# A Performer attention with two dense layers: seven products for six more pairs of the first block

## The chip, the cores and the metric

The kernel runs on one core of one Trainium2 chip. The metric is the device time of one execution in microseconds, the median of several runs. Of the engines, PE (TensorE) multiplies, ACT (ScalarE) and DVE (VectorE) work element by element, POOL (GpSimd) does a few subtractions and issues some DMAs, and SP (SyncE) issues the other DMAs. Each engine takes its instructions in order; an instruction may wait on semaphores of the others.

## The reference

Linear attention with random features, then two dense layers over 2304 tokens of width 512 with 2048 features:

```python
q_p, k_p = (phi(q_s), phi(k_s))          # phi: exp(x @ omega.T - |x|^2/2 - max) / sqrt(m)
num = einsum('bhsm,bhmd->bhsd', q_p, einsum('bhsm,bhsd->bhmd', k_p, v))
x = num / (q_p . sum(k_p) + 1e-06)       # 2304 x 512
h = x @ w_in;  x = (max(h, 0) + alpha * min(h, 0)) @ w_out      # layer 0
h = x @ w_in2; x = (max(h, 0) ** 2) @ w_out2                    # layer 1
```

The weights come as 8-byte numbers and the products need more than one rounded factor, so the kernel splits every operand into a high part (fp32r) and the rest, and takes three matmuls per product: high by high, high by rest, rest by high.

## The kernel before, in words

Attention comes first: k steps, then q steps, which write the tokens x. Layer 0 then goes over 3 blocks k of 768 tokens, and in each over 8 pairs p of two groups of 128 features; one such pass is a *turn* (0 to 7 in block 0). A turn has first products, features and second products.

The **first products** h = w1 x of a pair are a 2 by 2 block product over halves of the width and of the block (i is the feature group, 384 tokens to a half). `plain` (L820) takes 8 products, `pair` (L870) takes Strassen's seven, whose right factors are quarters B of x or differences T1 to T4 of quarters, and whose left factors are quarters A of w1 or sums S1 to S4. `multiply` (L767) is one product: 6 matmuls of 384 columns. Block 0 uses `plain` for all of its pairs, blocks 1 and 2 use `pair`. The rounded quarters are xh (ACT, L439) and xl (DVE, L442).

The **features**: ACT copies h from PSUM to c, or to a scaled copy s that DVE then adds to another h (`c<-h,sg,s`, L805, in `pair` only); DVE bends c (L810); ACT rounds it to gh (L792); DVE takes the rest gl (L816).

The **second products** y = w2 g (`mm2`, L950, L963) of a pair are spread over the turn of the next pair: after the products of a turn come as many of ten parts as `FILL` says, first those of i=1 (gh and both parts of w2), then i=1 with gl, then i=0. In a plain turn the first part comes after the first product, in a turn of seven after the second.

The **weights** of block 0 are made while it runs, and stored for the later blocks. A *unit* n makes w1 of pair n and w2 of pair n-1 and lies in turn n-1. It has four raws (a and b for w1; p and q for w2, i=1 and i=0): POOL issues the DMA of the 8-byte words (`Raw`, L122); ACT scales the high word in place (`scale_high`, L132) and writes the scaled low word as 16-bit numbers (L141) and the high word as f16 (L142) into the two halves of `rest`; DVE shifts the high word to t (L146) and merges t and rest to wf (L150). DVE makes the sums S (L168); ACT rounds wf to w (L229), DVE takes the rest (L232), SP stores both. Units are divided into 18 stages, and at each product the kernel issues the stages that are due (`upto`), so that weight operations stand between feature operations in the queues of ACT and DVE. Raws of block 0 are read into the part of x that no token fills at the time, three at a time; a new DMA is issued when a raw is merged.

Of the kernel before, what the change touches and what calls it, by code (L numbers as in the profile page):

```python
# [12 lines left out]
I16 = mybir.dt.int16  # L13
# [7 lines left out]
P = 128  # L21
# [39 lines left out]
def tile_performer_moe(ctx, tc, qt, kt, qn, kn, vn, omt, w1i, w1o, al, w2i, w2o, out):  # L61
# [113 lines left out]
    def made():  # L175
# [93 lines left out]

        yield  # L270
        for n, (n1, n2) in enumerate(UNITS[:NPAIR + 1]):
# [3 lines left out]
            todo = [[] for _ in range(STAGES)]  # L275
            if n1:
# [5 lines left out]
                todo[3] += [lambda: merge(a)] + [b.scale_low] * (n < 2)  # L282
                todo[4] += [b.shift] + [b.scale_low] * (n > 1)
# [93 lines left out]
    tp = making_room.enter_context(tc.tile_pool(name="tp", bufs=1, side="right", reuse_waits="tile"))  # L377
    tiles["wf1"] = wb.tile([P, 8, QW], F32, name="wf1")
# [995 lines left out]
```

## Time and profile before

| | us |
|---|---|
| median of 3 runs | 878.29 |
| lowest and highest | 878.25, 878.85 |
| profiled execution | 878.17 |
| its span in the trace | 876.4 |

In the profiled execution PE is busy 870.8 us, DVE 666.5, ACT 518.3 and POOL 88.9, at the full granted clock throughout. Attention ends near 139 us; block 0 of layer 0 lies from about 125 to 261 us. All times of the trace are microseconds from the start of the span; a row of a timeline gives the start, the length, and in brackets how long the engine had been idle and what it had waited for.

### The profile page before, as it was taken

Reading aid. Unit: us, or ns where it says so; the run is one execution under the profiler, and the core shown is the slowest. Engines: PE = TensorE matmul, PEld = TensorE weight load, DVE = VectorE, ACT = ScalarE, POOL = GpSimd, SP = SyncE. Lnnn points to the kernel's source line nnn. Section 1 sums busy time; section 2 is a strip of 40 time slices with the busy share of each in tenths; the row PEclk is TensorE's granted clock in tenths of the full one; section 3 lists DMA queues with packets and bytes.
Section 4 is the critical chain, followed back from the end, with each engine's and each line's share of the span. In section 5 each row is a group of like instructions: output and inputs, shape, how many; then the busy total and the mean of one; then the engine's idle time right before and its main releaser. Section 6 shows DMA issues by size and latency. Waiting matters only on the chain.

```text
span 876.4 us, 17518 instructions
## 1 busy us (share of the span) xinstructions
PE 870.8 (99%) x6848; PEld 807.5 (92%) x6848; DVE 666.5 (76%) x1095; ACT 518.3 (59%) x1023; POOL 88.9 (10%) x134
## 2 busy tenths in 40 slices
PE   9999999999999999999999999999999999999998
PEld 7998889999999999999999999998899988999887
DVE  4778987787777677797887875669965699757685
ACT  6889896888866566677667643335423245333442
POOL 6642321111101000001000000000000000000000
PEclk9999999999999999999999999999999999999999
DMA  8544316788835899948999966767687687876873
GB/s 286 187 137 160 111 38 217 264 314 307 291 157 211 327 384 412 370 145 304 402 390 393 357 243 189 252 260 282 239 300 250 209 325 258 289 254 219 309 258 142
DMA packets 86898, 228.76 MB, mean 261 GB/s; under 512 B 6688, under 2 KB 19360, under 8 KB 81824
## 3 DMA queue, kind: packets, MB, share of 16 engines
q1 hardware_dynamic: 77248, 192.21, 61.1%
q0 software_dynamic: 9216, 33.56, 10.8%
q10 hardware_dynamic: 352, 1.87, 0.6%
q8 instruction: 54, 0.88, 0.4%
q14 instruction: 28, 0.23, 0.1%
HBM read 170.47 MB, written 57.15 MB: 260 GB/s over the span
## 4 chain that ended last, share of the span: by engine, by line
PE 97%; ACT 2%; DMA 0%; DVE 0%; issue 0%; ACTq 0%; POOLq 0%
PE h L767 30%; PE y L963 22%; PE sumc L1153 11%; PE spare L767 10%; PE suma L1153 9%; PE h L532 4%; PE o L578 2%; PE t L539 2%; PE t L652 2%; PE o L684 2%; PE t L671 1%; PE t L526 1%; ACT e L557 0%; DMA x<-in_w2i 0%; PE h L1153 0%
## 5 line engine op out<-in xcount | busy, mean ns | idle before, releaser
L767 PE MATMUL h<-xh,w 128*128 128x384 f32 x1040 | 295.3, 337 | 0.3 <-ACT s L792 0.3
L767 PEld LDWEIGHTS h<-xh,w 128*128 128x128 f32 x1040 | 190.9, 188 | 3.3 <-ACT s L792 0.7
L963 PE MATMUL y<-gh,w 128*128 128x512 f32 (+1 forms) x768 | 175.4, 337 | 0.1
L767 PE MATMUL h<-xl,w 128*128 128x384 f32 x520 | 174.6, 336 | 0.0
L963 PEld LDWEIGHTS y<-gh,w 128*128 128x128 f32 x768 | 131.1, 188 | 11.6 <-ACT gh L792 0.5
L963 PE MATMUL y<-gl,w 128*128 128x512 f32 (+1 forms) x384 | 103.4, 337 | 0.0
L1168 ACT CAST gh<-g 128x768 fp32r<-128x768 f32 x72 | 56.9, 833 | 74.1 <-PE suma L1153 33.1
L767 PEld LDWEIGHTS h<-xl,w 128*128 128x128 f32 x520 | 97.7, 188 | 2.7
L767 PE MATMUL spare<-xh,w 128*128 128x384 f32 x336 | 90.9, 334 | 0.0
L1153 PE MATMUL sumc<-w,gh 128*128 128x512 f32 (+1 forms) x296 | 76.6, 379 | 0.0
L1170 DVE TENSOR_TENSOR gl<-g,gh 128x768 fp32r<-128x768 f32 x72 | 65.7, 953 | 14.3 <-PE suma L1153 7.1
L963 PEld LDWEIGHTS y<-gl,w 128*128 128x128 f32 x384 | 67.5, 188 | 9.3
L792 ACT ACTIVATE c<-h,sg_sb 128x384 f32<-128x384 f32 x48 | 28.0, 583 | 59.1 <-PE h L767 59.0
L767 PEld LDWEIGHTS spare<-xh,w 128*128 128x128 f32 x336 | 61.3, 188 | 0.2
L1153 PEld LDWEIGHTS sumc<-w,gh 128*128 128x128 f32 x296 | 52.8, 189 | 9.3
L545 DVE TENSOR_REDUCE mx<-h 128x8 f32<-128x1024 f32 x36 | 44.1, 1224 | 21.7 <-PE h L532 21.2
L810 DVE SCALAR_TENSOR_TENSOR c<-c,al_sb 128x768 f32<-128x768 f32 x48 | 48.6, 1013 | 12.3 <-ACT c L792 12.3
L767 PE MATMUL spare<-xl,w 128*128 128x384 f32 x168 | 56.1, 334 | 0.0
L1153 PE MATMUL suma<-w,gh 128*128 128x512 f32 x216 | 52.4, 391 | 0.0
L792 ACT ACTIVATE gh<-c,sg_sb 128x768 fp32r<-128x768 f32 x48 | 45.1, 940 | 8.3 <-DVE c L810 8.0
L150 DVE CUSTOM_DVE_ANT_0 wf<-t,rest 128x1024 uint16<-128x1024 uint16 x58 | 40.0, 690 | 11.8 <-ACT rest L142 9.8
L1153 PE MATMUL sumc<-w,gl 128*128 128x256 f32 x280 | 48.5, 282 | 0.0
(112 smaller groups left out, 1480.3 us busy)
## 6 DMA issues: line engine op xcount, KB each, us to landing
w<-k SPq DMA_DIRECT2D x99, 512.0 KB, 5.1
w<-k SPq DMA_DIRECT2D x39, 1024.0 KB, 4.6
w<-k SPq DMA_DIRECT2D x26, 896.0 KB, 8.5
k<-ms SPq DMA_DIRECT2D x36, 512.0 KB, 7.4
k<-w SPq DMA_DIRECT2D x7, 1792.0 KB, 6.2
x<-in_w1i POOLq DMA_DIRECT2D x16, 512.0 KB, 4.4
x<-in_w1o POOLq DMA_DIRECT2D x16, 512.0 KB, 7.3
k<-w SPq DMA_DIRECT2D x16, 512.0 KB, 6.0
```

The costliest lines, as they stand in the source:

```text
L150: nc.vector.tensor_tensor(out=self.out.bitcast(I32), in0=self.t, in1=self.rest, op=ALU.add)
L532: nc.tensor.matmul(pj[:, j, c, :], raws[key][rows, c, :], om[rows], start=True, stop=True)
L539: nc.tensor.matmul(o[rows, 2 * c:2 * c + 2], sqt[:, c, rows], pick, start=True, stop=True, skip_group_check=True)
L545: nc.vector.reduce_max(out=mx, in_=pj, axis=AX.X)
L578: nc.tensor.matmul(acc[b][ms, g, k * W:(k + 1) * W], es[i][rs, h % 2, h // 2, ms], vas[i % 4][rs, h], start=first and k == 0, stop=last, s ...
L767: nc.tensor.matmul(out, w[:, u, a, cs], tiles[v, b][:, kc], start=start and kc == 0 and j == 0, stop=stop and kc == 1 and j == 2, skip_gro ...
L792: nc.scalar.mul(out=to, in_=of, mul=sg_sb[:, 2 * p + i:2 * p + i + 1])
L810: nc.vector.scalar_tensor_tensor(out=c, in0=c, scalar=slope, in1=c, op0=ALU.mult, op1=ALU.max)
L963: nc.tensor.matmul(y[a0 // 512][:, a0 % 512:a0 % 512 + a1 - a0], u[:, i, c * P:(c + 1) * P], v[:, i, ts], start=first and j == 0 and a0 % ...
L1153: nc.tensor.matmul(to[c] if v == 3 or banks else to[c][:, :QW], (l if v == 2 else h)[:, r, c * P:(c + 1) * P], both(r) if v == 3 else w[:, ...
L1168: nc.scalar.copy(out=h[:, r], in_=f[:, r])
L1170: nc.vector.tensor_tensor(out=l[:, r], in0=f[:, r], in1=h[:, r].bitcast(F32), op=ALU.subtract)
```

## The change

- **Turns 2 to 7 of block 0 use `pair`** (`whole` is n < 2), with the fill table of seven products. Turns 0 and 1 stay `plain`.
- **T1 to T4 of block 0** are made by POOL in place of quarters of x (`apart`, 128x768 each, at q steps 12 to 15), and rounded by ACT and DVE in turns 1 and 2 (`SPLIT`).
- **Units from 2 on** are no longer built from the 18 stages, but by `evenly`, which names what comes at each product (`STEPS`). A21 is not rounded any more, so one cast and one rest are 256 columns wide instead of 512.
- **The joined words**: `scale_low` writes the scaled low word as whole 32-bit numbers into one of two buffers, `joined` or `ma`, and `sign` then writes the f16 high word over the upper half of each. `sign` waits for that write.
- **Raws** of units from 2 on are read into the `ms` buffers instead of x (`blk` is None); the two of w2 of pair 0 go to a buffer of gl and to a new one, `rx`.
- Blocks 1 and 2 use one table `NEXT`, and issue their weight stages over 52 products instead of 50.

```diff
+APART = {12: 4, 13: 6, 14: 5, 15: 3}
 CAST = 11
 STAGES, SHORT = 18, 10
+STEPS = (2, 5, 7, 10, 12, 15, 17)
...
+            if Raw.count in places:
+                raw = places[Raw.count]
+            elif blk is None:
+                raw = tiles["double"][k].bitcast(I32)
+            else:
+                raw = x[:, blk].rearrange("p c n -> p (c n)").bitcast(I32)[:, k * 2 * DM:(k + 1) * 2 * DM]
...
-        def scale_low(self):
+        def scale_low(self, to=None):
 
             if self.beside:
                 nc.scalar.mul(out=self.low, in_=self.low.bitcast(U32), mul=2.0 ** -29)
                 return
-            self.rest = tp.tile([P, DM], I32, name="rest")
-            part = lambda dtype, n: self.rest.bitcast(dtype).rearrange("p (n w) -> p n w", w=2)[:, :, n]
-            nc.scalar.mul(out=part(I16, 0), in_=self.low.bitcast(U32), mul=2.0 ** -29)
-            nc.scalar.copy(out=part(F16, 1), in_=self.high.bitcast(F32))
+            self.rest = tiles["joined"] if to is None else to
+            nc.scalar.mul(out=self.rest, in_=self.low.bitcast(U32), mul=2.0 ** -29)
+            if to is None:
+                self.sign()
+
+        def sign(self):
+
+            part = self.rest.bitcast(F16).rearrange("p (n w) -> p n w", w=2)[:, :, 1]
+            nc.scalar.copy(out=part, in_=self.high.bitcast(F32))
...
+        def evenly(n, n1, n2, todo):
+
+            def put(step, *what):
+                todo[STEPS[step]] += what
+
+            joined = tiles["joined"], tiles["single"].bitcast(I32)
+            put(3 if n > 2 else 1, trail)
+            put(3, *[trail] * (n == 2))
+            if n1:
+                a, b = used[n, 0, 0], used[n, 0, 1]
+                put(0, a.scale_high)
+                put(1, lambda: a.scale_low(joined[0]), a.sign, a.shift, lambda: read_out(a))
+                put(2, lambda: merge(a), b.scale_high, lambda: b.scale_low(joined[1]), b.shift)
+                put(3, b.sign, lambda: read_out(b), lambda: cast1(n1, A11, S1))
+                put(4, lambda: merge(b), lambda: sums((1, 3)), lambda: sums((2, 4)), lambda: rest1(n1, A11, S1))
+            if n2:
+                p, q = (lambda: used[n, 1, 1]), (lambda: used[n, 1, 0])
+                put(3, lambda: p().scale_high())
+                put(4, lambda: p().scale_low(joined[0]))
+            if n1:
+                put(4, lambda: cast1(n1, A22, A11))
+            if n2:
+                put(4, lambda: p().sign(), lambda: p().shift(), lambda: read_out(p()), lambda: q().scale_high())
+            if n1:
+                put(4, lambda: cast1(n1, S1, S3), lambda: rest1(n1, A22, A11))
+                put(5, lambda: rest1(n1, S1, S3))
+            if n2:
+                put(5, lambda: q().scale_low(joined[1]), lambda: q().sign(), lambda: merge(p()),
+                    lambda: q().shift(), lambda: read_out(q()))
+            if n1:
+                put(5, lambda: cast1(n1, S3, 8))
+            if n2:
+                put(6, lambda: cast2(n2, 1))
+            if n1:
+                put(6, lambda: rest1(n1, S3, 8),
+                    lambda: keep(n1, 0, slice(0, 7), ring[n1[1] % 2][0][:, :, A22:]))
+            if n2:
+                put(6, lambda: merge(q()), lambda: rest2(n2, 1), lambda: cast2(n2, 0),
+                    lambda: tail.append(lambda: rest2(n2, 0)))
...
+            if n > 1:
+                evenly(n, n1, n2, todo)
+                n1 = n2 = None
...
+    INSTEAD = {T1: (0, 0), T3: (0, 1), T2: (1, 1), T4: (1, 0)}
+    SPLIT = {(1, 0): [(cast, T2)], (1, 1): [(rest, T2)], (1, 2): [(cast, T1)], (1, 3): [(rest, T1)],
+             (1, 4): [(cast, T3)], (1, 5): [(rest, T3)], (2, 1): [(cast, T4)], (2, 2): [(rest, T4)]}
+
+    def in_place(_, n):
+
+        return quarter(0, *INSTEAD[n])
+
+    def apart(n):
+
+        of = {T1: (T3, T1), T3: (T2, T3), T2: (T2, T1), T4: (T4, T2)}[n]
+        a, b = (in_place(0, m) for m in of)
+        nc.gpsimd.tensor_tensor(out=in_place(0, n), in0=a, in1=b, op=ALU.subtract)
...
+            places[4] = mp["gp"].tile([P, 2, NB], F32R, name="gl").rearrange("p i n -> p (i n)").bitcast(I32)[:, :2 * DM]
+            places[5] = rx.tile([P, 2 * DM], I32, name="rx")
...
+                    if s in APART:
+                        apart(APART[s])
...
-        first = (layer, k) == (0, 0)
-        steps = stepping.pop() if stepping else plain(p) if first else pair(layer, p)
+        first, whole = (layer, k) == (0, 0), n < 2
+        if n == 0:
+            ask(ENDS[0], None)
+        steps = stepping.pop() if stepping else plain(p) if whole else pair(layer, p)
...
+            for what, operand_ in SPLIT.get((n, m), ()):
+                what(0, operand_, in_place)
...
-            for _ in range(FILL[0 if first else 1][m]):
+            for _ in range(FILL[0 if whole else 1][m]):
```

The instructions on ACT in one turn in the middle of block 0, before (w_0, w_1: the two w1 and w2 buffers; c and gh with h: features):

```order
L792 ACTIVATE c<-h,sg_sb 128x384
L229 CAST w_0_101<-wf_99 128x512 x2
L141 ACTIVATE rest<-x 128x512
L142 CAST rest<-x 128x512
L229 CAST w_1_2695<-wf_100 128x512
L792 ACTIVATE gh<-c,sg_sb 128x768
L792 ACTIVATE c<-h,sg_sb 128x384
L132 ACTIVATE x<-x 128x512
L141 ACTIVATE rest<-x 128x512
L142 CAST rest<-x 128x512
L132 ACTIVATE x<-x 128x512
L792 ACTIVATE gh<-c,sg_sb 128x768
```

Here gh follows a single cast of w2 (`w_1_2695`), and the next raw's work stands between the two gh.

ACT in the changed kernel, from the end of one turn into the next (s: the scaled copy for `c<-h,sg,s`; ms: raws; L138, L146, L153 are scale_high, the low write and `sign`):

```order
L244 CAST w_0_104<-wf_101 128x512 x2
L864 ACTIVATE gh<-c,sg_sb 128x768
L864 ACTIVATE s<-h,sg_sb 128x384
L138 ACTIVATE ms_2698<-ms_2698 128x512
L864 ACTIVATE gh<-c,sg_sb 128x768
L146 ACTIVATE joined<-ms_2698 128x512
L153 CAST joined<-ms_2698 128x512
L864 ACTIVATE s<-h,sg_sb 128x384
L138 ACTIVATE ms_2699<-ms_2699 128x512
L146 ACTIVATE ma<-ms_2699 128x512
L153 CAST ma<-ms_2699 128x512
L244 CAST w_0_102<-wf_100 128x512
```

The casts of w2 (`w_0_104`) now stand directly ahead of gh, and all work on raws a and b comes behind it, with s between.

DVE in a middle turn before, from the first sum:

```order
L168 TENSOR_TENSOR wf_99<-wf_99 128x256 x4
L146 TENSOR_SCALAR t<-x 128x512
L150 ISA wf_100<-t,rest 128x1024
L232 TENSOR_TENSOR w_0_101<-wf_99,w_0_101 128x512
L810 SCALAR_TENSOR_TENSOR c<-c,al_sb 128x768
L232 TENSOR_TENSOR w_0_101<-wf_99,w_0_101 128x512
L232 TENSOR_TENSOR w_1_2695<-wf_100,w_1_2695 128x512
L146 TENSOR_SCALAR t<-x 128x512
L150 ISA wf_100<-t,rest 128x1024
L810 SCALAR_TENSOR_TENSOR c<-c,al_sb 128x768
```

Both merges (L150) come within a few rows of the sums, with two rests and a bend between.

DVE in the changed kernel, from the `c<-h,sg,s` after the fifth product to the one after the seventh:

```order
L877 SCALAR_TENSOR_TENSOR c<-h,sg_sb,s 128x384
L161 ISA wf_100<-t,ma 128x1024
L179 TENSOR_TENSOR wf_100<-wf_100 128x256 x4
L247 TENSOR_TENSOR w_0_102<-wf_100,w_0_102 128x512
L157 TENSOR_SCALAR t<-ms_2697 128x512
L247 TENSOR_TENSOR w_0_102<-wf_100,w_0_102 128x256
L247 TENSOR_TENSOR w_0_102<-wf_100,w_0_102 128x512
L161 ISA wf_101<-t,joined 128x1024
L157 TENSOR_SCALAR t<-ms_2698 128x512
L882 SCALAR_TENSOR_TENSOR c<-c,al_sb 128x768
L877 SCALAR_TENSOR_TENSOR c<-h,sg_sb,s 128x384
L247 TENSOR_TENSOR w_0_102<-wf_100,w_0_102 128x512
```

Behind `c<-h,sg,s` stand the sums, three rests and the merge of p.

The end of a turn in the changed kernel on DVE (the turn before the rows above), from the shift of q:

```order
L157 TENSOR_SCALAR t<-ms_2697 128x512
L882 SCALAR_TENSOR_TENSOR c<-c,al_sb 128x768
L877 SCALAR_TENSOR_TENSOR c<-h,sg_sb,s 128x384
L247 TENSOR_TENSOR w_1_103<-wf_100,w_1_103 128x512
L161 ISA wf_101<-t,ma 128x1024
L247 TENSOR_TENSOR w_0_104<-wf_101,w_0_104 128x512
```

The merges of p and q (L161 to `wf_101`) now stand behind the sums, three rests and a bend, at the turn's end.

## Rows read from the trace of the kernel before

**Rows 1.** The page, part 1: busy time and share of each engine.
```profile
PE 870.8 (99%) x6848; PEld 807.5 (92%) x6848; DVE 666.5 (76%) x1095; ACT 518.3 (59%) x1023; POOL 88.9 (10%) x134
```

**Rows 2.** PE timeline: start, length, engine, line, operation, names, shapes, count [idle before].
```profile
140.46 0.51 PE L767 MATMUL h<-xh,w 128*128 128x384 f32 x2
...
143.58 0.34 PE L767 MATMUL h<-xh,w 128*128 128x384 f32 x1
...
159.54 0.33 PE L767 MATMUL h<-xh,w 128*128 128x384 f32 x1
...
260.50 0.33 PE L767 MATMUL h<-xh,w 128*128 128x384 f32 x1
```

**Rows 3.** ACT timeline, end of turn 3 and start of turn 4 (same columns).
```profile
190.92 0.62 ACT L229 CAST w<-wf 128x512 fp32r<-128x512 f32 x1
191.43 0.94 ACT L792 ACTIVATE gh<-c,sg_sb 128x768 fp32r<-128x768 f32 x1
192.34 0.58 ACT L792 ACTIVATE c<-h,sg_sb 128x384 f32<-128x384 f32 x1
192.82 0.67 ACT L132 ACTIVATE x<-x 128x512 f32<-128x512 f32 x1
...
194.08 0.76 ACT L142 CAST rest<-x 128x512 f16<-128x512 f32 x1
194.70 0.68 ACT L132 ACTIVATE x<-x 128x512 f32<-128x512 f32 x1
195.28 0.92 ACT L792 ACTIVATE gh<-c,sg_sb 128x768 fp32r<-128x768 f32 x1
```

**Rows 4.** ACT groups, 30 to 500 us: busy us, mean ns | idle before.
```profile
L137 ACT ACTIVATE x<-x 128x512 int32<-128x512 uint32 x4 | 3.0, 758 | 0.0
```

**Rows 5.** DVE groups by line and shape, 30 to 500 us.
```profile
L805 DVE SCALAR_TENSOR_TENSOR c<-h,sg_sb,s 128x384 f32<-128x384 f32 x45 | 27.7, 615 | 13.6 <-PE h L767 5.1 <-ACT s L792 5.0 <-ACT ms L229 2.3
...
L232 DVE TENSOR_TENSOR ma<-wf,ma 128x256 fp32r<-128x256 f32 x15 | 6.3, 419 | 1.8 <-ACT ma L229 1.8
```

**Rows 6.** DVE timeline of turns 3 and 4.
```profile
192.18 0.42 DVE L146 TENSOR_SCALAR t<-x 128x512 int32<-128x512 int32 x1
192.64 0.69 DVE L150 CUSTOM_DVE_ANT_0 wf<-t,rest 128x1024 uint16<-128x1024 uint16 x1
193.25 1.01 DVE L810 SCALAR_TENSOR_TENSOR c<-c,al_sb 128x768 f32<-128x768 f32 x1
194.18 1.01 DVE L816 SCALAR_TENSOR_TENSOR gl<-c,sg_sb,gh 128x768 fp32r<-128x768 f32 x1
...
195.67 0.69 DVE L150 CUSTOM_DVE_ANT_0 wf<-t,rest 128x1024 uint16<-128x1024 uint16 x1
196.45 0.43 DVE L146 TENSOR_SCALAR t<-x 128x512 int32<-128x512 int32 x1
196.79 1.01 DVE L816 SCALAR_TENSOR_TENSOR gl<-c,sg_sb,gh 128x768 fp32r<-128x768 f32 x1
...
200.83 0.69 DVE L232 TENSOR_TENSOR w<-wf,w 128x512 fp32r<-128x512 f32 x1 [0.42 <-ACT w L229]
201.44 1.55 DVE L168 TENSOR_TENSOR wf<-wf 128x256 f32<-128x256 f32 x4
```

**Rows 7.** ACT timeline, turn 1: its first weight operation.
```profile
143.81 0.67 ACT L132 ACTIVATE x<-x 128x512 f32<-128x512 f32 x1
```

**Rows 8.** POOL timeline: one L521 of a q step, and the DMA after attention.
```profile
114.95 1.04 POOL L521 TENSOR_TENSOR sqt<-raw 128x512 f32<-128x512 f32 x1 [3.21 <-PE t L539]
...
141.57 0.55 POOL L122 DMA_DIRECT2D x<-in_w1o  x1 [0.30 <-POOL wf L154]
```

**Rows 9.** DMA issues from 120 to 260 us: count, KB each, median us to landing.
```profile
x<-in_w1o POOLq DMA_DIRECT2D x14, 512.0 KB, 7.6
x<-in_w1i POOLq DMA_DIRECT2D x12, 512.0 KB, 4.0
```

**Rows 10.** ACT groups from 143 to 261 us: rounding a token quarter.
```profile
L439 ACT CAST xh<-x 128x768 fp32r<-128x768 f32 x2 | 1.6, 824 | 0.0
```

More of the change, by code (lines that the diff above doesn't have):

```diff
@@ L12 @@
 F16 = mybir.dt.float16
-I16 = mybir.dt.int16
 I32 = mybir.dt.int32
@@ L100, in tile_performer_moe @@
     tiles = {}
+    places = {}
     class Raw:
@@ L196, in merge, with read_out @@
             raw.merge()
+            if raw in raws:
+                read_out(raw)
+        def read_out(raw):
             raws.remove(raw)
@@ L281, in made @@
                 todo[2] += [a.shift, b.scale_high]
-                todo[3] += [lambda: merge(a)] + [b.scale_low] * (n < 2)
-                todo[4] += [b.shift] + [b.scale_low] * (n > 1)
+                todo[3] += [lambda: merge(a), b.scale_low]
+                todo[4] += [b.shift]
                 todo[5] += [lambda: merge(b), lambda: cast1(n1, A11, S1)]
@@ L303, in made @@
                 todo[10] += [lambda: raw(0).scale_high()]
-                todo[11] += [lambda: raw(1).shift()] + [lambda: raw(0).scale_low()] * (n < 2)
+                todo[11] += [lambda: raw(1).shift(), lambda: raw(0).scale_low()]
                 todo[12] += [lambda: merge(raw(1))]
-                todo[13] += [lambda: raw(0).scale_low()] * (n > 1)
                 todo[14] += [lambda: cast2(n2, 1)]
@@ L1033, in tile_performer_moe @@
             if first and turn:
-                upto((p + 1) * STAGES + STAGES * (m + 1) // 8 + 1, ENDS[0], 0)
-            elif layer == 0 and k and turn * 7 + m > (0, 5, 3)[k]:
-                upto(end_of(ENDS[k - 1]) + (end_of(ENDS[k]) - end_of(ENDS[k - 1])) * (turn * 7 + m - (0, 5, 3)[k]) // (0, 50, 49)[k],
+                upto((p + 1) * STAGES + STAGES * (m + 1) // (8 if whole else 7) + 1, ENDS[0], None)
+            elif layer == 0 and k and turn * 7 + m > 3:
+                upto(end_of(ENDS[k - 1]) + (end_of(ENDS[k]) - end_of(ENDS[k - 1])) * (turn * 7 + m - 3) // (0, 52, 49)[k],
                      ENDS[k], k)
-            elif layer == 0 and k and m == (0, 5, 3)[k]:
+            elif layer == 0 and k and m == 3:
                 ask(ENDS[k], k)
             elif (layer, k, turn) == (0, 1, 0) and m < 2:
-                onward(ENDS[0], 0)
-            for blk, at in ((n // NPAIR, turn * (8 if first else 7) + m), (n // NPAIR - 1, NPAIR * 7 + turn * 7 + m)):
-                table = NEXT[0 if blk == 0 else 1]
-                at -= (NPAIR - 1) * (8 if blk == 0 and first else 7)
-                if blk == 0 and not first:
-                    at += 1
+                onward(ENDS[0], None)
+            for what, operand_ in SPLIT.get((n, m), ()):
+                what(0, operand_, in_place)
+            for blk, at in ((n // NPAIR, turn * 7 + m), (n // NPAIR - 1, NPAIR * 7 + turn * 7 + m)):
                 if 0 <= blk < BLOCKS:
-                    for what, operand_ in table.get(at, ()):
+                    for what, operand_ in NEXT.get(at - (NPAIR - 1) * 7, ()):
                         what((blk + 1) % BLOCKS, operand_)
```

21 lines of the change are left out of this document (8 added, 13 removed).

## Prediction

> **What bounds the kernel now.** I read the page's first part, then PE's timeline in block 0 of the first layer, then the timelines of ACT and DVE beside it. PE is busy 870.8 of 876.4 us [rows 1], and in block 0 its rows follow each other without a gap [rows 2]: 18 matmuls of 384 columns from 140.46 to 143.58, 0.1733 us each, and six turns from 159.54 to 260.50, 16.83 us each. So before the change a matmul removed is time gained, as long as PE stays dense. The profiled execution is 878.17 us, the median 878.29; I sum against 878.2.
>
> **What the change takes from PE.** A plain turn has 8 products of 6 matmuls, a turn of seven products has 7. Six turns (pairs 2 to 7) lose 6 matmuls each: 6 x 0.1733 = 1.04 us, so a dense turn becomes 15.79 us, and all six are worth 6.24 us. The order of the changed program has these 36 matmuls less, so this gain is there if PE never waits. The question is whether ACT and DVE can now make weights and features in 15.79 us per turn.
>
> **The ring of ACT and DVE.** In the new order both engines serve weights and features alternately, in order. Two waits close a ring in every turn from 3 to 7. ACT's copy s of the fifth product stands behind all its raw work of the turn; DVE's c<-h waits for that s, and behind it in DVE's queue stands the rest of the turn up to the merge of the last raw (q). ACT's cast of w for i=0 waits for that merge, and right behind that cast stands gh, which PE's first `y<-gh,w` of the turn needs. So one lap of the ring is the least length of a turn. I count start to start, from rows.
>
> ACT, from the cast of w (i=0) to the end of s: casts of w 0.51, gh 0.91, s 0.48, a scaling of high words 0.58, the old half-word f16 copy 0.62 [rows 3]. The new whole-word write of the low part: rows of the same form (L137) last 0.758 [rows 4]. Its f16 copy (`sign`) now waits for exactly that write, so the write counts with its whole length and a hand-over, 0.78, where today's 16-bit write gives way before its end. The lap: cast 0.51, gh 0.91, s 0.48, scale a 0.58, gh 0.91, low a 0.78, sign 0.62, s 0.48, scale b 0.58, low b 0.78, sign 0.62, cast A11 0.51, scale p 0.58, s 0.61 to its end = 8.95 us.
>
> DVE, from c<-h to the end of the merge of q: c<-h 0.615 long [rows 5], 0.53 start to start (other rows lose 0.08 to the overlap with the next); the merge of b 0.69 and 0.03, as the first sum waits for it; four sums 1.55 less 0.08 = 1.47; rests of 512 columns 0.61, of 256 columns 0.419 [rows 5] less 0.08 = 0.34; t 0.34 when nothing waits for it (196.45 to 196.79); a merge with a t that waits for it 0.78; bend 0.93 [rows 6]. The lap: 0.53, 0.72, 1.47, rest A11 0.61, t p 0.34, rest A22 0.34, rest S1 0.61, merge p and wait 0.78, t q 0.34, bend 0.93, c<-h 0.53, rest S3 0.61, merge q 0.72 = 8.53 us.
>
> Together **17.48 us per turn**, 1.69 more than the 15.79 of PE, and even 0.65 more than today's 16.83. PE itself is not in this lap: its fifth product ends 5.2 us after its first y (three products of 1.04, three fills of 0.69, which are 1536 columns each), ACT's s is due 7.5 us after. PE then stands once per turn, before its first `y<-gh,w`. Today there is no such ring: gh waits for a bend only, and ACT's casts and DVE's rests have the length of the turn.
>
> Is the wait of `sign` for its predecessor that dear on ACT? No row of before has an ACT instruction that waits for the one before it. On DVE there are such rows: the merge at 192.64 starts 0.46 after its t of 0.42, where t alone gives way after 0.34 [rows 6]. I take the whole length, and the other end is the 0.65 of today's low write (0.13 less, twice in a lap).
>
> The Trainium skill speaks for the dear end: Perfetto Trace Analysis, section "DVE / Act Engine Instruction (TENSOR_ADD, Activation, etc)", says that the end that the profiler reports is the acknowledged write with its semaphore update, so what waits for it cannot start inside the overlap. The DVE rows agree; for ACT no row does. By the page the total is the one below, by free overlap 1.5 us less.
>
> **Turn 1, where the new order begins.** The first raws of unit 2 were in x early: ACT scales the first at 143.81 [rows 7]. Now they go to ms, which is free only after the last attention step, so their DMAs start about where POOL's next one starts today, at 141.57 [rows 8], and words of w1i take 4.0 us [rows 9]: 145.6. ACT then has in its queue: scale 0.58, cast xh 0.74 (0.824 long [rows 10], less the overlap), gh 0.91, c 0.48, cast w 0.51, low 0.78, sign 0.62, xh 0.74, c 0.48, scale b 0.68 to its end: 152.1. DVE's t of b follows (0.34), then the new xl of T1 (about a bend, 0.87 to 0.93), then the rest of w for i=0 (0.69): 154.0. PE wants that rest at T1 = 142.71 (159.54 less one turn) plus five products (5.2) and six fills (4.2) and one matmul: 152.35. **Stall 1.65 us.** PE's sixth product, and with it ACT's third c, moves to about 155.9; ACT's nine operations behind it (c 0.48, low 0.78, A22 0.3, sign 0.62, scale 0.58, S1 0.51, low 0.78, sign 0.62, S3 0.61 = 5.3) and DVE's last rests and merges bring the merge of q to about 163.0. The rest of w (i=1) ends at 164.0, where PE wants it at 163.55: 0.5 us. Turn 2's lap has no first gh but one more xh, about 17.5; its gh is ready at 163.0 + 17.5 + 0.51 + 0.94 = 181.95, where PE is at 163.8 + 15.79 = 179.6: 2.35 us.
>
> **What is hidden.** POOL's four subtractions: L521's 128x512 takes 1.04 us [rows 8], so 1.56 at 768 columns; POOL has 3.21 us idle before each L521 of a step, and the results are wanted in turn 1. Cost 0, at most 0.5 us if one pushes a sqt. Casts and rests of T1 to T3 in turn 1 are in the sum above. The smaller A22 cast and rest (256 columns) are in the lap. SP has the same writes of kept weights. Turn 7 makes no first-product weights, so its lap lacks the merges of a and b, the sums and four rests (some 5 us), and gh of pair 7 is in time for turn 8. Blocks 1 and 2 keep their products, and their weight operations are spread over 52 steps instead of 50; `sign` costs ACT 0.13 for each raw there, and ACT is busy 518 of 876 us [rows 1]: 0.
>
> **Sum.** -6.24 + 1.65 + 0.5 + 2.35 + 4 x 1.69 (turns 4 to 7) = +5.0: **883.2 us**.
>
> **Bounds.** Without the wait of `sign`: -0.26 a turn, six turns, 881.7. Without the late DMAs of turn 1 as well, the first two stalls: -2.15, 879.5. Intervals of one form differ by some 0.03 between rows (scaling 0.58 and 0.61); were all 26 of a lap 2% shorter, -1.75 more: 877.8. Upwards: q's raw takes over a's buffer, so its DMA starts about 5 us into the lap and lands at 12.6 with 7.6 us for w1o [rows 9]. From then scale, S1, c and its write end at 14.3, DVE's bend wants c at 14.7. So up to 8.0 us it is hidden; every us beyond costs one per turn, 5 in all.
>
> **Rivals.**
> 1. The ring is not as tight as I count it, and PE stays dense: 878.2 - 6.2 = 872.0, and up to 876.5 with the stalls that begin in turn 1 (1.65, 0.5, 2.35). For it: ACT's and DVE's busy sums per turn (about 14.5 and 14.1 us by the same intervals) are under 15.79, so each engine alone would do. Against it: the lap would have to lose 1.7 of 17.48 us, 10%, in operations whose rows are constant to 0.03. Chance 0.15.
> 2. The lap comes out near 16.9 (no price for `sign`, every interval at its lower end): turns cost what they cost before, the gain of 6.24 is just eaten: 877 to 879.9. Chance 0.15.
> 3. The DMA of q is late in each turn, as it reads beside the writes of kept weights: at 9 us one us in each of five laps, +5, 888. Chance 0.05.
> 4. The program doesn't do what it says: excluded by the order, which has the 36 matmuls less.
>
> **How the numbers follow.** Forecast 883.2 (ring binds, 880.1 to 887.5): 0.65. A measurement of this kernel can tell some 0.2% from no change, so the bounds are 876.5 and 880.0. Faster 0.15 (rival 1), same 0.15 (rival 2 and the low end of the bounds), slower 0.70 (forecast and rival 3). The range leaves out rival 1 and rival 3: 876.6 to 887.5, which keeps 0.80.
>
> **What would show it.** Right: PE rows with idle time before the first `y<-gh,w` of turns 3 to 7, released by ACT's gh, about 1.7 us each, and one in turn 1 before an i=0 y, released by DVE's rest; turns of 17.5 us between first products of pairs; `sign` starting 0.78 after the low write. Wrong: turns of 15.8 us with PE dense (rival 1), of 16.8 (rival 2), or ACT's scale of q with idle time released by a DMA of in_w1o (rival 3). The forecast falls if ACT's gh is issued well before DVE's merge of q ends, since the ring has then another way round.

## The result and the profile after

The changed kernel takes **884.61 us** (median of 6 runs, 882.45 to 888.04), the kernel before beside it 878.95 us (6 runs, 878.25 to 879.29): **1.0069 times as long, 95% interval 1.0047 to 1.0091**. The forecast was 883.2 (876.6 to 887.5) and slower. The profiled execution of the changed kernel took 886.25 us, with a span of 884.5.

The first line of the page after, against [rows 1]: PE, DVE, ACT and POOL by busy us, share of the span, instructions.

```profile
PE 869.9 (98%) x6812; PEld 802.9 (91%) x6812; DVE 677.0 (77%) x1117; ACT 519.9 (59%) x1027; POOL 96.7 (11%) x138
```

PE has the 36 matmuls less. But busy time fell by only 0.9 us, not 6.24, and the span grew. In this execution PE ran for a while at half clock, which puts back 3.4 us (below), and busy time on this page contains modelled ends of matmuls, so a share of 98% does not say "dense". The timeline does. PE of the changed kernel: start, length, names, shapes, count, and the idle time before; the first y of turn 1, the rows in which PE had waited, and the first h of turns 2, 3 and 8.

```profile
147.85 0.86 PE L1035 MATMUL y<-gh,w 128*128 128x512 f32 x4
...
157.85 0.51 PE L1035 MATMUL y<-gh,w 128*128 128x512 f32 x1 [1.17 <-DVE w L247]
...
165.09 0.33 PE L839 MATMUL h<-xh,w 128*128 128x384 f32 x1
...
181.72 0.34 PE L839 MATMUL h<-xh,w 128*128 128x384 f32 x1
...
185.54 0.74 PE L1035 MATMUL y<-gh,w 128*128 128x512 f32 x2 [1.36 <-ACT gh L864]
...
202.60 0.73 PE L1035 MATMUL y<-gh,w 128*128 128x512 f32 x2 [1.06 <-ACT gh L864]
...
220.17 0.97 PE L1035 MATMUL y<-gh,w 128*128 128x512 f32 x4 [1.38 <-ACT gh L864]
...
237.20 0.97 PE L1035 MATMUL y<-gh,w 128*128 128x512 f32 x4 [1.02 <-ACT gh L864]
...
255.13 0.96 PE L1035 MATMUL y<-gh,w 128*128 128x512 f32 x4 [1.37 <-ACT gh L864]
...
268.88 0.33 PE L839 MATMUL h<-xh,w 128*128 128x384 f32 x1
```

Once per turn PE stands before the same instruction, the first `y<-gh,w`, and always for ACT's gh; in turn 1 it stands for DVE's rest of w. From one such y to the next it is 17.06, 17.57, 17.03 and 17.93 us. The six turns 2 to 7 take 268.88 - 165.09 = **103.79 us, where before took 100.96** [rows 2]; 6 x 15.79 would have been 94.7. PE's two largest waits from 140 to 270 us, by who was waited for (total us, times, longest):

```profile
PE y L1035 <- ACT gh L864: 6.2, 5, 1.4
PE y L1035 <- DVE w L247: 1.2, 1, 1.2
```

And why gh is late: ACT in the lap from 201.09 to 218.67 (same columns), and DVE's rows of the same lap.

```profile
201.09 0.62 ACT L244 CAST w<-wf 128x512 fp32r<-128x512 f32 x1 [2.04 <-DVE wf L161]
201.62 0.93 ACT L864 ACTIVATE gh<-c,sg_sb 128x768 fp32r<-128x768 f32 x1
...
204.30 0.68 ACT L146 ACTIVATE joined<-ms 128x512 int32<-128x512 uint32 x1
205.01 0.78 ACT L153 CAST joined<-ms 128x512 f16<-128x512 f32 x1
...
209.10 0.56 ACT L864 ACTIVATE s<-h,sg_sb 128x384 f32<-128x384 f32 x1
...
213.00 0.70 ACT L138 ACTIVATE ms<-ms 128x512 f32<-128x512 f32 x1 [0.96 <-DMA ms<-in_w1o]
...
218.67 0.62 ACT L244 CAST w<-wf 128x512 fp32r<-128x512 f32 x1 [1.62 <-DVE wf L161]
```

```profile
209.70 0.62 DVE L877 SCALAR_TENSOR_TENSOR c<-h,sg_sb,s 128x384 f32<-128x384 f32 x1 [1.85 <-ACT s L864]
...
214.22 0.69 DVE L247 TENSOR_TENSOR w<-wf,w 128x512 fp32r<-128x512 f32 x1 [0.43 <-ACT w L244]
...
217.95 0.69 DVE L161 CUSTOM_DVE_ANT_0 wf<-t,ma 128x1024 uint16<-128x1024 uint16 x1
```

This is the ring, read from one row to the next: the cast of w starts at 201.09, ACT works without a gap to the end of s at 209.66, DVE's c<-h has waited 1.85 us for it, DVE works on to the merge that ends at 218.64, and the next cast, which has waited for that merge, starts at 218.67 with gh right behind it. ACT's half is 8.57 us, DVE's 8.94. Of DVE's, 0.43 is a wait that begins on ACT (the row of 213.00): the words of q had not landed.

**A part that lies elsewhere.** The first y of turn 1 comes at 147.85. In the kernel before it starts at 143.76, behind the last h of [rows 2]'s first turn:

```profile
143.76 0.86 PE L963 MATMUL y<-gh,w 128*128 128x512 f32 x4
```

These 4.09 us arise in attention, where PE's order is the same in both kernels, and they have two sources. The larger one lies at 22 us. PE's row and the engines' busy time by stretches of 4 us (stretch, its length, busy us and instructions of PE, PE's loads, DVE, ACT, POOL, then the granted clock as a share of 2.4 GHz, DMA share, GB/s):

```profile
22.27 0.60 PE L599 MATMUL h<-om,raw 64*128 64x128 f32 x6 [0.68 <-issue]
```

```profile
20.00:24.00 4.00, 3.32 (x78) 2.91 (x74) 1.87 (x4) 3.81 (x13) 1.99 (x3) 1.00 0.48 149
24.00:28.00 4.00, 4.00 (x71) 3.69 (x69) 3.25 (x9) 3.00 (x10) 2.10 (x3) 0.64 0.71 208
28.00:32.00 4.00, 4.00 (x60) 3.76 (x60) 0.92 (x3) 2.57 (x9) 1.73 (x3) 0.51 0.32 87
```

PE paused for 0.68 us, and then ran most of two stretches at half clock, 1.2 GHz. By the granted clock 1.44 and 1.96 us of full speed are missing there ((1 - 0.64) x 4 and (1 - 0.51) x 4); with the pause that is 4.08. Row against row it is 4.05: PE is 0.43 ahead of the kernel before at 20.66 (there 21.09) and 3.62 behind it at 33.91 (there 30.29).

The smaller source is part of the change. POOL's first subtraction in place, one of DVE's xl beside it, and PE behind them:

```profile
102.58 1.81 POOL L526 TENSOR_TENSOR x<-x 128x768 f32<-128x768 f32 x1
```

```profile
103.50 1.70 DVE L501 TENSOR_TENSOR xl<-x,xh 128x768 fp32r<-128x768 f32 x1
```

```profile
107.08 1.06 PE L719 MATMUL t<-ident,eq 128*128 128x128 f32 x8 [0.42 <-DVE mx L618]
```

The three xl ahead of this one take 0.95 us each. This one, which starts while POOL subtracts, takes 1.70; the mx behind it comes late, and PE waits 0.42 us for it. From there on PE is 4.09 behind (108.08, there 103.99), 0.46 more than ahead of it. The kernel before has no such wait, and the traces of all the runs below have it. That the subtraction lengthens the xl is argued from these rows; no run takes it away.

The six executions have 882.45 us at a mean clock of 1.000, 883.09 at 0.999, 884.87 and 884.35 at 0.998, 886.25 at 0.996 and 888.04 at 0.994; the shortest, at full clock, is 4.2 us over the shortest of before. Turns 1 to 7 are 4.29 longer (122.07 from the first h of turn 1, 1.04 ahead of its first y, to that of turn 8; before 117.78), with the 0.46 in attention 4.75. So the change itself costs some 4.2 to 4.8 us; the rest of the 5.7 between the medians goes with the clock. For this reason the experiments below are compared by the stretch from the first h of turn 2 to that of turn 8, in which the granted clock was 1.00 unless something else is said: **103.79 in the changed kernel, 100.96 before**.

### The profile page after: what moved, and what is told of

It reads as the page before. It is cut to its first block, busy times and chain, and to the rows that moved or that the text cites. A ratio compares the mean times of both kernels' runs of the same rounds, so it can differ in the third digit from the quotient of the medians.

```text
span 884.5 us, 17465 instructions
## 1 busy us (share of the span) xinstructions
PE 869.9 (98%) x6812; PEld 802.9 (91%) x6812; DVE 677.0 (77%) x1117; ACT 519.9 (59%) x1027; POOL 96.7 (11%) x138
## 3 DMA queue, kind: packets, MB, share of 16 engines
q0 software_dynamic: 9216, 33.56, 11.3%
## 4 chain that ended last, share of the span: by engine, by line
PE 85%; ACT 7%; DVE 5%; issue 2%; DMA 1%; POOL 0%; ACTq 0%
PE h L839 24%; PE y L1035 17%; PE sumc L1225 11%; PE spare L839 10%; PE suma L1225 9%; PE h L599 4%; PE o L645 2%; PE t L606 2%; PE t L719 2%; PE o L751 2%; ACT gh L864 1%; DVE w L247 1%; ACT ms L138 1%; PE t L738 1%; DVE wf L161 1%
## 5 line engine op out<-in xcount | busy, mean ns | idle before, releaser
L839 PE MATMUL h<-xh,w 128*128 128x384 f32 x1016 | 287.2, 337 | 1.0 <-ACT s L864 0.6
L839 PEld LDWEIGHTS h<-xh,w 128*128 128x128 f32 x1016 | 186.3, 188 | 5.3 <-DVE c L877 1.4
L839 PE MATMUL h<-xl,w 128*128 128x384 f32 x508 | 170.4, 335 | 0.0
L839 PEld LDWEIGHTS h<-xl,w 128*128 128x128 f32 x508 | 95.5, 188 | 2.0
L877 DVE SCALAR_TENSOR_TENSOR c<-h,sg_sb,s 128x384 f32<-128x384 f32 x66 | 40.6, 615 | 27.1 <-ACT s L864 16.5
L864 ACT ACTIVATE s<-h,sg_sb 128x384 f32<-128x384 f32 x66 | 38.0, 576 | 32.6 <-PE h L839 32.5
L624 ACT ACTIVATE e<-h,nb 128x128 f32<-128x128 f32 x144 | 39.2, 382 | 16.8 <-DVE nb L619 16.7
```

Source lines behind the costliest of these rows:

```text
L624: nc.scalar.activation(out=e[:, c, :], in_=pj[:, c, :], func=AF.Exp, bias=nb[:, c:c + 1])
L839: nc.tensor.matmul(out, w[:, u, a, cs], tiles[v, b][:, kc], start=start and kc == 0 and j == 0, stop=stop and kc == 1 and j == 2, skip_gro ...
L864: nc.scalar.mul(out=to, in_=of, mul=sg_sb[:, 2 * p + i:2 * p + i + 1])
L877: nc.vector.scalar_tensor_tensor(out=c[:, ts], in0=b, scalar=sign, in1=s, op0=ALU.mult, op1=ALU.add)
```

## The experiments

Theory A is the prediction's: the lap of ACT and DVE through gh sets the turn. Its rivals: one engine has simply too much work; PE is dense and the loss lies elsewhere; the DMA of q sets the turn.

### Work doubled inside and outside the ring

Run e2_rest_twice_in_ring makes one rest of w (DVE, 0.61) twice within DVE's half of the lap:

```diff
-  put(4, ..., lambda: rest1(n1, A11, S1))
+  put(4, ..., lambda: rest1(n1, A11, S1),
+      lambda: rest1(n1, A11, S1))
```

> Edit: the rest of A11 (DVE, 512 columns, 0.61 us) is done twice, right where it stands: between the s of the fifth product and the merge of q. Ring theory: each lap grows by 0.61, turns 3 to 7 from 17.4 to 18.0, the stretch from turn 1 to turn 8 by 5 to 6 x 0.61 = 3.0 to 3.7 us to about 125.5. Rival (load): the same 3.7, so this run tells only together with the next. Rival (PE or the DMAs set the turn): 0.

Run e3_rest_twice_outside makes the same operation on the same engine, as often, behind the merge of q, where nothing on the way to gh waits for it:

```diff
-  lambda: tail.append(lambda: rest2(n2, 0)))
+  lambda: tail.append(lambda: (low(second(n2, 1, 0), f2[:, 0], second(n2, 0, 0)), rest2(n2, 0))))
```

> Edit: the rest of w2 for i=0 (DVE, the same operation and size, 0.61 us) is done twice where it stands, after the shift of b, where DVE then waits 1.85 us for ACT's s. Ring theory: the copy falls into that wait: 0, within 0.3 us in the whole stretch (122.1). Rival (load): +3.7, as for the copy in the ring.

The first h of turn 2 and of turn 8 on PE, first in e2, then in e3 (there with DVE's c<-h of the lap):

```profile
161.76 0.33 PE L840 MATMUL h<-xh,w 128*128 128x384 f32 x1
...
270.13 0.33 PE L840 MATMUL h<-xh,w 128*128 128x384 f32 x1
```

```profile
162.77 0.33 PE L839 MATMUL h<-xh,w 128*128 128x384 f32 x1
...
266.60 0.33 PE L839 MATMUL h<-xh,w 128*128 128x384 f32 x1
```

```profile
207.34 0.62 DVE L877 SCALAR_TENSOR_TENSOR c<-h,sg_sb,s 128x384 f32<-128x384 f32 x1 [1.12 <-ACT s L864]
```

Inside the ring: 108.37, 4.58 more. Outside: 103.83, 0.04 more, though DVE does as much: it waits for s all the same, only 0.7 us less than in the changed kernel. This pair alone puts "DVE has too much work" aside: **what counts is where the work stands**. That the inside one cost more than the 3.0 to 3.7 expected has two reasons in the rows (first y of three turns, a stretch of 3 us, and ACT's scaling of q in e2):

```profile
200.70 0.69 PE L1036 MATMUL y<-gh,w 128*128 128x512 f32 x1 [1.35 <-ACT gh L865]
...
219.05 0.97 PE L1036 MATMUL y<-gh,w 128*128 128x512 f32 x4 [0.84 <-ACT gh L865]
...
237.77 0.50 PE L1036 MATMUL y<-gh,w 128*128 128x512 f32 x1 [1.37 <-ACT gh L865]
```

```profile
201.00:204.00 3.00, 3.00 (x11) 2.82 (x11) 2.85 (x5) 2.85 (x5) 0.00 (x0) 0.50 1.02 429
```

```profile
230.60 0.68 ACT L138 ACTIVATE ms<-ms 128x512 f32<-128x512 f32 x1 [2.11 <-DMA ms<-in_w1o]
```

The bare lap is 17.04 (run e9 below), with one more rest 17.65. The lap from 200.70 took 18.35: a PE wait of 1.35 us was followed by a stretch at half clock. The lap from 219.05 took 18.72, at full clock: ACT waited 2.11 us for q's words.

### The ring cut

Run e1_cast_behind_gh keeps every operation and moves one: the cast of w for i=0 is issued in the next turn, behind gh and s, so that gh no longer stands behind a wait for DVE.

```diff
-  put(3 if n > 2 else 1, trail)
+  put(0 if n > 2 else 1, trail)
+  put(3, *[trail] * (n > 2))
...
-  ... lambda: cast2(n2, 0),
+  ... *([lambda: cast2(n2, 0)] if n == NPAIR else [lambda: tail.append(lambda: cast2(n2, 0))]),
```

> Edit: the cast of w2 for i=0 is issued in the next turn, behind gh and s, instead of ahead of gh; nothing else. Ring theory (gh waits for the merge of q, since that cast stands ahead of it): the wait of 1.0 to 1.4 us before the first y<-gh of turns 3 to 7 goes; ACT's part of the lap loses gh and s (0.84 + 0.46), so a lap is 17.40 - 1.3 = 16.1 us and bounds the turn weakly; turns 3 to 7 about 16.1, the stretch from turn 1 to turn 8 122.1 - 5 x 1.3 = 115.5 us, below the 117.8 of before. Rival (load: ACT and DVE have too much to do in a turn, wherever it stands): the wait moves to another place, the stretch stays at 122 within 1 us.

It took 879.87 us, and 99.99 in the stretch, 3.8 less than the changed kernel, where 6.6 were expected. PE's longest wait in total from 140 to 262 us:

```profile
PE y L1037 <- DVE w L247: 2.5, 6, 1.3
```

The wait for gh is gone altogether, so it was the cast ahead of gh that carried it. But the lap from 197.83 to 214.57 is still 16.74 us: the merge of q still releases that cast, and the cast an s further on in ACT's queue, and s the next merge. The ring is shorter, not open. The expectation had put this shorter lap at 16.1 us, and had left out that q's words come late here too: ACT waits 0.88, 0.97 and 0.67 us for them in three turns.

Run e5_ring_cut_twice takes away from ACT's half what stands ahead of the s of the fifth product as well: the cast of A11 and the scaling of p go behind it.

```diff
-  put(3, b.sign, lambda: read_out(b), lambda: cast1(n1, A11, S1))
+  put(3, b.sign, lambda: read_out(b))
+  put(4, lambda: cast1(n1, A11, S1))
...
-  put(3, lambda: p().scale_high())
-  put(4, lambda: p().scale_low(joined[0]))
+  put(4, lambda: p().scale_high(), lambda: p().scale_low(joined[0]))
```

> Edit: as in the run with the cast of w2 behind gh, and ACT's cast of A11 and the scaling of p stand behind the s of the fifth product instead of ahead of it. Ring theory: ACT's part of the lap between two merges of q loses 0.52 + 0.55 us, laps of 16.2 to 16.7 become 15.1 to 15.7, under PE's 15.79; PE dense but for 0.3 us a turn, so the stretch from turn 2 to turn 8, 103.8 in the changed kernel and 100.0 with the first edit alone, is 95 to 97 us. Rival (load: the same operations, so the same turns as with the first edit alone): 100.

878.89 us, 100.05 in the stretch: nothing won over e1, for two reasons. In turn 2 PE waits for ACT's c, and the turn takes 17.73 us instead of e1's 16.65. And turns 3 to 7 fall only from 83.34 to 82.32 (dense they would be 79); what ACT waits for from 160 to 262 us in e5 fits that. PE's row of turn 2, then ACT's wait:

```profile
163.70 0.45 PE L841 MATMUL h<-xh,w 128*128 128x384 f32 x1 [1.21 <-ACT c L866]
```

```profile
ACT ms L138 <- DMA ms<-in_w1o: 6.4, 5, 2.0
```

In the changed kernel the same wait was 1.2 us in all. With the ring cut, the raw of q is late in every turn: its transfer can start only when ACT and DVE have finished with a, whose buffer it takes.

Run e6_and_early_rest adds to e5 that in turn 1 the second of two pending rests of w is issued at step 1, not at step 3:

```diff
-  put(0 if n > 2 else 1, trail)
+  put(0 if n > 2 else 1, *[trail] * (1 if n > 2 else 2))
```

> Edit: as the run before, and in turn 1 the rest of w2 for i=0 is issued ahead of the shift of a, not behind the shift of b. Theory: PE's wait of 1.2 to 1.3 us in turn 1 goes (its cast is done 3 us before PE wants it), turn 1 from 18.3 to 17.0 us, the rest as in the run before; in all some 874 to 876 us against 878.3 of before, and runs that spread as little as those of before (0.1%), if the spread of the changed kernel (0.6%) comes from clock drops at its waits. Rival: turn 1 stays at 18.3 since ACT's late start moves the wait elsewhere.

Turn 1 fell to 16.82 us (18.29 in the changed kernel), the wait for DVE's w is gone, and the stretch is 99.92. In all 879.76 us (11 runs) against 878.70, ratio 1.0006 (0.9988 to 1.0023), where 874 to 876 were expected: the changed kernel with its ring cut twice and turn 1 mended is just the kernel before. The spread expected, 0.1%, did not come either: 877.03 to 881.43, at mean clocks of 0.999 and 1.000, so clock drops are not all of the spread.

### A fourth buffer for the raws

Run e9_changed_and_fourth takes the changed kernel as it is, and gives the raws of pairs 2 to 6 a fourth buffer (the room of ta and tb, two sums of token quarters that pairs 2 to 6 don't use).

```diff
-  raw = tiles["double"][k].bitcast(I32)
+  room = [*tiles["double"][:3], tiles["fourth"]]
+  raw = room[(Raw.count - 6) % 4 if Raw.count < 26 else (Raw.count - 26) % 3].bitcast(I32)
...
-  while order and len(raws) < 3 and ...:
+  while order and len(raws) < (4 if room[0] is None and Raw.count < 26 else 3) and ...:
```

> Edit: the changed kernel with the fourth buffer alone, order of ACT and DVE unchanged. Ring theory: laps lose only the two waits for the DMA (0.96 and 0.22 us, of which 0.5 and 0.2 show in a lap), laps of 17.0 instead of 17.0 to 17.9, the stretch from turn 2 to turn 8 103.8 - 0.5 to -1.5 = 102.3 to 103.3. If the DMA of q were what sets the turn: 97 or less.

886.06 us (with a pause and a low clock between 22 and 32 us, as above); the stretch is 103.22, as expected. PE's first y of two turns in e9:

```profile
202.80 0.50 PE L1036 MATMUL y<-gh,w 128*128 128x512 f32 x1 [1.04 <-ACT gh L865]
...
219.83 0.72 PE L1036 MATMUL y<-gh,w 128*128 128x512 f32 x2 [1.06 <-ACT gh L865]
```

The laps are now 17.04, 17.03 and 17.05 us, all alike. **17.04 is the bare ring**, and the half microsecond in some laps of the changed kernel was the DMA. The transfer was a small addition there, and the ring was the bound.

Run e11_a11_behind_s adds to e9 only the move of A11's cast and of p's scaling behind s; the cast of w stays ahead of gh.

```diff
-  put(3, b.sign, lambda: read_out(b), lambda: cast1(n1, A11, S1))
+  put(3, b.sign, lambda: read_out(b))
+  put(4 if n > 2 else 3, lambda: cast1(n1, A11, S1))
...
-  put(3, lambda: p().scale_high())
+  put(4 if n > 2 else 3, lambda: p().scale_high())
```

> Edit: the changed kernel with the fourth buffer, and in units from 3 on ACT's cast of A11 and the scaling of p behind the s of the fifth product; the cast of w2 stays ahead of gh. Ring theory: two operations of 0.52 and 0.55 us leave ACT's part of the lap, so the laps of 17.04 become 15.97, 0.18 above PE's 15.79; PE's wait before the first y<-gh falls from 1.0 to 0.2 us or less in turns 4 to 6, and the stretch from turn 3 to turn 7 from 68.7 to 64.4 us or a little less. Rival (it is the cast's place ahead of gh alone that counts): laps stay at 17.0.

878.53 us. First h of turns 4 to 7 on PE:

```profile
195.35 0.33 PE L841 MATMUL h<-xh,w 128*128 128x384 f32 x1
...
211.47 0.34 PE L841 MATMUL h<-xh,w 128*128 128x384 f32 x1
...
227.59 0.33 PE L841 MATMUL h<-xh,w 128*128 128x384 f32 x1
...
243.68 0.34 PE L841 MATMUL h<-xh,w 128*128 128x384 f32 x1
```

Turns of 16.12, 16.12 and 16.09, where 15.97 was expected: two operations of together about 1.1 us were taken out of the lap, and it lost 0.93. So the lap can be reckoned from its parts, here to within 0.15 us.

Run e8_fourth_buffer has all of it: e6, the fourth buffer, and for pair 2 the old place of A11 and p (in turn 1, ahead of the wait of turn 2 shown for e5).

> Edit: as the run with the ring cut twice and the early rest, and units 2 to 6 read their raws into four buffers instead of three (the fourth lies in ta and tb, which are free until turn 6), so that q's DMA is issued as soon as the q of the turn before is read; in turn 1 alone A11 and p keep their old place. Theory (after the cuts the DMA of q sets the turn: ACT waited 1.0 to 2.0 us for it in each of turns 2 to 6): those waits go, turns 2 to 6 fall from 15.7 to 17.8 to 15.8 to 16.1, the stretch from turn 2 to turn 8 from 100 to 96 to 97.5 (turn 7 still has three buffers), in all 875 to 877 us. Rival (ACT and DVE are still the lap): 100 as before.

**873.93 us (6 runs, 873.21 to 874.75) against 879.41: ratio 0.9933 (0.9916 to 0.9951).** It beats both kernels. PE's busy time in one turn, first of the changed kernel, then of e8 (columns as for the stretches above):

```profile
181.70:199.30 17.60, 16.24 (x92) 14.58 (x91) 14.86 (x27) 14.32 (x25) 2.47 (x5) 1.00 0.79 290
```

```profile
208.86:224.59 15.73, 15.73 (x92) 14.66 (x91) 14.35 (x26) 14.26 (x25) 1.58 (x3) 1.00 0.92 321
```

The same 92 matmuls in 15.73 us instead of 17.6, PE without a gap, while DVE and ACT are busy nearly as long. Four turns take 15.73 each, the stretch 95.69 (expected 96 to 97.5). Against e6, turn 2 gives 0.9 us of that (17.79 to 16.90; which of the two edits does it, no run tells), and turns 3 to 7, in which only the buffer differs, give 3.35 (82.14 to 78.79). The prediction's rival 1, 872.0, was out of reach for the changed kernel, not for its mathematics.

### The price of sign's wait

Run e7_half_words and run e10_half_words_and_fourth let the low write fill 16-bit halves, so that sign has nothing to wait for: e7 on the changed kernel, e10 on e9.

```diff
-  nc.scalar.mul(out=self.rest, in_=self.low.bitcast(U32), mul=2.0 ** -29)
+  nc.scalar.mul(out=self.rest.bitcast(I16).rearrange("p (n w) -> p n w", w=2)[:, :, 0], in_=self.low.bitcast(U32), mul=2.0 ** -29)
```

> Edit: the changed kernel, but the low part is written as 16-bit numbers into the lower halves as before, so that sign does not wait for it; buffers and order unchanged. By the prediction's price for that wait (0.13 us, twice in a lap, six turns) the stretch from turn 2 to turn 8 falls from 103.8 by 1.5; by the trace of the changed kernel (the write 0.71 from start to start, 0.65 today) by 2 x 0.06 x 6 = 0.7 us. If the wait were free: 0.

e7 decides nothing: 888.79 us, a stretch of 106.88, with a granted clock of 0.58 from 220 to 224 us, and longer waits for q's DMA, among which a gain of this size can't be read.

> Edit: the run before with half words, so that sign does not wait for the low write, now without DMA waits in between. Price of the wait by the trace: 2 x 0.06 us a lap, so 0.6 to 0.7 us less than the run before in the stretch from turn 2 to turn 8; by the prediction's 0.13 it would be 1.5.

e10, without those DMA waits and at full clock: 881.42 us, a stretch of 102.45, which is 0.77 less than e9 (expected 0.6 to 0.7). The same two waits of PE as shown for e9:

```profile
198.88 0.50 PE L1037 MATMUL y<-gh,w 128*128 128x512 f32 x1 [0.87 <-ACT gh L866]
...
215.79 0.73 PE L1037 MATMUL y<-gh,w 128*128 128x512 f32 x2 [0.93 <-ACT gh L866]
```

Laps of 16.88, 16.91 and 16.88 against 17.04: against the half-word write, the whole-word write with sign's wait costs 0.15 per lap, some 0.075 for each of two raws. It is not the price of the wait alone, since the two writes differ in length too (0.68 us as whole words, 0.79 as half words).

### The step-by-step order itself

Runs e4_stages and e4b_stages give pairs from 2 on the order of stages that pair 1 has, in place of the one placed step by step. In e4 a merge reads the joined words of the next raw, so its second-product weights aren't the reference's; e4b has the low write of q behind the merge of p instead.

```diff
-  if n > 1:
-      evenly(n, n1, n2, todo)
-      n1 = n2 = None
...
-  if n < 2:
-      todo[4] += [trail]
-      todo[7] += [trail]
+  todo[4] += [trail]
+  todo[7] += [trail]
```

> Edit: units from 2 on are built from the 18 stages as before, not step by step; products, differences by POOL, buffers of the raws and joined words stay as changed (with one joined buffer instead of two). gh then stands ahead of the cast that waits for the merge of q. Ring theory: no lap through gh, so PE's wait before the first y<-gh of a turn is under 0.3 us, turns of 15.8 to 16.5, the stretch from turn 1 to turn 8 113 to 117 us; against it, four merges in a row now share one joined buffer, which may make a lap of its own. Rival (load): 122 or more, since DVE and ACT have 0.2 to 0.3 us more to do in a turn (A21 is rounded again).

> Edit: units from 2 on built from the 18 stages, as in the earlier run, but the low words of q are written after the merge of p (in that run before it, so that p was merged with q's words). gh stands ahead of the cast that waits for the merge of q. By that run: PE no longer waits at y but 1.1 us a turn at the third product, for ACT's s, which now stands behind casts and low writes that wait for merges; the stretch from turn 2 to turn 8 about 104 to 106 us. Ring theory as I first had it (only the lap through gh counts): 96 to 98.

Both expectations failed. e4 took 886.96 us and 105.71 in the stretch (some 95 to 99 expected; its granted clock was 0.91 from 160 to 180 us), e4b 895.99 and 113.0 (104 to 106 expected; its granted clock was below 0.85 in several pieces of 4 us). PE's wait in e4 from 160 to 268 us (in e4b the same wait has 9.7 us), and one turn of e4b at full clock, from first h to first h (columns as above):

```profile
PE h L835 <- ACT s L860: 6.7, 5, 2.3
```

```profile
220.25:238.35 18.10, 16.27 (x92) 14.58 (x90) 14.70 (x26) 14.65 (x24) 2.11 (x4) 1.00 0.77 275
```

No wait for gh worth naming, but a longer one for s. What makes s late was not tested: ACT's waits for merges of joined words are short in e4b (3.0 us in nine), and there ACT also waits for PE's h (12.0 in five) and for DVE's bend (8.5 in seven). So "without this lap PE is dense" was too simple: these orders have other waits. Between the orders that give the reference's weights, the step-by-step one is the better: 17.05 to 17.57 us for turns 3 to 6 of the changed kernel, 18.10 for this turn of e4b.

## Why the prediction was right, point by point

**The gain of PE**: right. The forecast's dense turn was 15.79 us; e8's dense turns are 15.73. It is there whenever nothing makes PE wait.

**The ring**: right as a mechanism, and shown: e2 and e3 (position of the same work), e1 (the wait for gh goes with the cast ahead of it) and e11 (about 1.1 us taken out of it, 0.93 gained). Its size was 17.48 in the forecast; the bare ring is 17.04 (e9), with q's late words 17.57. The ACT half measured 8.57 instead of 8.95, DVE's 8.40 instead of 8.53 in a lap without DMA wait (227.25 to 235.65). Of ACT's 0.38, 0.15 lies in the two low writes and as much in the two gh, which give way after 0.84 and 0.83 us (201.62 and 203.47), not 0.91. So PE's waits before the first y were 1.02 to 1.38 us and not 1.7, and turns 3 to 7 took 17.05 to 17.92.

**The wait of sign**: the right kind; the write that it waits for was taken too long. The forecast took 0.78 from [rows 4] as the start-to-start time of the low write; it is 0.71, since here the write lasts 0.68 and not 0.758. sign starts at 205.01, when the write that began at 204.30 has ended at 204.98, where other rows of ACT start about 0.09 before their predecessor ends (cast and gh at 201.09 and 201.62). The Trainium skill, Perfetto Trace Analysis, section "DVE / Act Engine Instruction (TENSOR_ADD, Activation, etc)", has the reported end at the acknowledged write; the ACT rows agree. Against the half-word write it is worth 0.15 per lap (e10), where the forecast said 0.26: over six turns 0.77, not 1.5.

**Turn 1**: wait of 1.17 us, turn longer by 1.46 (18.29 against 16.83), forecast 1.65. e6 takes it away by an earlier rest, so it was DVE's rest indeed. The late start of the raws shows in ACT's first scaling of turn 1, and its releaser is the DMA, as forecast:

```profile
149.54 0.67 ACT L138 ACTIVATE ms<-ms 128x512 f32<-128x512 f32 x1 [1.54 <-DMA ms<-in_w1i]
```

The first y of this turn is itself 4.09 later than before, so this row is to be compared with 145.6 + 4.09 = 149.7.

**Turns 2 to 7**: turn 2 took 16.63, that is 0.84 over 15.79 (forecast 0.5, but as a wait for DVE's rest, which PE's rows don't have there), turns 3 to 7 together 8.21 over (forecast 2.35 + 4 x 1.69 = 9.11). With turn 1 the excess is 10.5, forecast 11.3. One part had no term: the last lap, up to turn 7's first y, is 17.93 (in e9 too), because DVE then also makes the quarter sum tb between a shift and a bend:

```profile
249.98 0.95 DVE L491 TENSOR_TENSOR tb<-x,ta 128x768 f32<-128x768 f32 x1
```

**POOL's subtractions**: priced at nothing, or 0.5 us if one pushes a sqt. They last 1.81 to 2.26 us instead of 1.56. By the rows above they cost PE some 0.46 us (argued, not tested), by a way that was not asked about: the xl of DVE beside the first of them.

**The DMA of q**: the step that failed, though it moved the total little. The forecast let the landing be hidden up to 8.0 us from its issue, as only DVE's bend was asked about. The rest of S1 stands ahead of that bend, by the forecast's own intervals at 12.96 us of the lap, and a landing at 12.6 ends S1's cast at 13.8: by the same reckoning the cover was 6.8 us. POOL issued it 5.0 us into the lap, as forecast:

```profile
206.08 0.53 POOL L128 DMA_DIRECT2D ms<-in_w1o  x1 [6.61 <-DVE gl L888]
```

But ACT wanted the words at 212.04, 5.96 us later, and got them at 213.00; right behind that scaling stands the cast of S1, whose rest on DVE waited 0.43. So the cover was some 6.5 us (6.92 to the landing less 0.43), not 8.0, and from there DVE's half grows; where ACT waited 0.22 for q's words (at 246.88), DVE's rest did not wait. And the forecast treated it as a rival to the ring; it is the next bound behind it (e5, e6): cutting the ring a second time won 1.0 us in turns 3 to 7, and the buffer 3.35 more (e8).

**The sum**: +4.29 over turns 1 to 7, forecast +5.0; with the 0.46 in attention 4.75. The medians differ by 5.66, and the longer executions are those with a lower clock, for which the forecast had no term. So a part of its closeness to the time is luck: the bare ring was priced 0.44 per lap too long, and q's late words, tb, the subtraction and the clock, none of them in the sum, made up for it.

**What stays open**: why PE pauses at some 22 us with nothing to wait for in the profile, and why only some of these pauses bring a low clock: e3 has one of 0.62 us without. Whether the change has a part in it no run here tells. The kernel before has executions with a low clock too, as one of 882.42 us at a mean clock of 0.996 and one of 885.82 at 0.992, but no trace of one was kept.

## What to carry to other kernels

Where two engines take turns in order, list who waits for whom once around and add the start-to-start times of one lap: if the lap is longer than the work of the engine that bounds the kernel, it can be the time, as it was here, though both engines were idle for a sixth of it. To test for it, do one operation twice, once inside the lap and once beside it. When the lap is cut, look for what was late behind it: here a transfer, for which a fourth buffer of 512 KB, in room that another phase had left unused, was enough. And a piece of work given to an idle engine is not free for that alone: look at what runs beside it.

## What the runs showed of the hardware that was not expected

A short wait of PE can be followed by a longer stretch at half clock: 0.68 us by eight at 0.64 and 0.51 on the mean (the changed kernel, 24 to 32 us), 1.35 us by 3 us at 0.50 (e2, 201 to 204 us). Other waits of the same length were not: 1.17 and 1.36 us in turns 1 and 3 of the changed kernel, where the granted clock stays at 1.00. A wait of PE on the path is thus not always worth only its own length.

DVE's xl (two inputs of 768 columns) took 1.70 us where it started during a subtraction of POOL of the same size, and 0.95 in the three steps before.
